# Gated linear attention with a convolved MLP on one core: the scores of all 24 chunks in 64x64 tiles of TensorE

## Chip, cores and metric

One core of a Trainium2 chip runs the whole kernel. The metric is the device time of one execution in microseconds, lower is better.

## What is computed

The reference is a gated linear attention over 4 batches, 8 heads, 768 tokens and 48 channels per head, followed by a three-tap convolution gate in a two-layer network:

```python
f = 1.0 / (1.0 + np.exp(-f_logit))
for t in range(S):
    state = f[:, :, t, :, None] * state + np.einsum('bhd,bhe->bhde', k[:, :, t], v[:, :, t])
    y[:, :, t] = np.einsum('bhd,bhde->bhe', q[:, :, t], state)
# y is laid out as x[b, t, 384], then:
h = np.maximum(x @ w_in, 0.0)                        # 384 -> 1024
conv_out[t] = sum(conv_w[k] * h[t + k - 1] for k in range(3))
out = (h * sigmoid(conv_out)) @ w_out                # 1024 -> 384
```

## The kernel before

The 768 tokens of a batch are cut into 6 chunks of 128, so there are 24 chunks, `n` = 0 to 23. Within a chunk the recurrence becomes matrix products. The running products of the gates scale k and q (`scaled_k`, `scaled_q`); the scores are k times q for every pair of tokens of the chunk; a mask keeps the keys that are not later than the query; the masked scores times v, and the carried state times q, give y. The state is carried on with a product of the turned k (`turned`, a transpose) and v (`state`).

The 8 heads stand in 4 pairs `p` (`NP = 4`); in a pair, head `j = 0` has its 48 channels on partitions 0 to 47 and head `j = 1` on partitions 64 to 111. All of the attention is in plain fp32, and a matmul in fp32 runs as two passes: the trace has two weight loads (LDWEIGHTS) and two MATMUL records for each.

The scores go to the PSUM tile `pa` (128 keys x 2 x 4 x 128 queries) in `scores`. There are two forms, chosen by `NA = 9`:

- For chunks 0 to 8 (line 346) one matmul for each pair and head, with all 128 keys as weights and all 128 queries streamed: 8 matmuls, 16 passes, in two tiles of the array of 64 rows x 128 columns.
- For chunks 9 to 23 (line 353) the 128 keys are cut into four strips of `G = 32`, and each strip is multiplied only with the queries from it on, so that 128, 96, 64 and 32 queries are streamed: 32 matmuls, 64 passes, in eight tiles of 64 rows x 32 columns. In every other pair the keys stand in reversed order (the host lays k and v out so), which puts the strip with 128 queries into the last column tile instead of the first.

VectorE (DVE) then copies the scores under a mask into `am` (`copy_predicated`, lines 357 and 360). For reversed keys the scaling of k must read its factor reversed in every other pair, so `scaled_k` is one DVE operation of 128x512 for chunks 0 to 8 (line 318) and two of 128x256 for the rest (line 321). The parts of `am` of the other pairs that the mask changes over from the one form to the other are cleared on GpSimd (POOL) ahead of chunks 9 and 10 (line 340).

The order of all work is written out by hand in the table `ORDER`: each entry lets one step run on to its next `yield`. The letters that matter here are K (`scaled_k`), a (`scores`: first the matmuls, then the masked copy), y (`values`, line 400: y from the masked scores, then from the state), k (`turned`, line 331), s (`state`, lines 373 and 378), m (`hidden`, line 456: the first layer of the network), r (`result`, lines 495 to 514: the second layer), j (`gated`), and I, J, H, O, P, S, which load and split the weights into two fp32r parts. Each engine works its own list strictly in this order. `pa` has one buffer, and so has the tile `py` that `values` fills.

Of the kernel before, what the change touches and what calls it, by code (L numbers as in the profile page):

```python
# [17 lines left out]
P = 128  # L18
# [1 line left out]

F_MIN = 2.0 ** -64
PN = 6
NA = 9
TS = 24
ON_POOL = ""
ORDER = """
# [10 lines left out]
P1 j0.2 S5 P2 m1.0 m1.0 p8 S0 F12 Q7 j0.0 a7 h1.0 L9 m1.1 s6 K8 S5 L10 s6 m0.7 Q8 m1.0 a7 y6 k8 P1 P1 m1.2 m0.5 m0.7  # L37
m1.3 k8 j0.2 P1 V9 m1.5 m0.6 h1.2 m1.2 m1.2 m0.4 p9 m1.5 m1.3 s7 P2 K9 P4 s7 P1 P4 j0.4 a8 y6 y6 m1.2 P4 P4 S2 m1.3 P1
F13 k9 p9 y7 k9 y7 m1.2 V8 m0.6 m1.4 j0.4 s7 m1.5 a8 m1.7 y7 m1.4 y7 m1.3 m1.4 F14 y8 m1.1 V11 m0.6 m0.7 y8 S1 x12 m1.3
a9 M10 t8 h1.4 L11 m1.5 S2 m1.2 Q9 P4 m1.4 G10 P4 O7 m1.5 P6 P6 a9 s8 j0.6 m1.4 j0.6 y8 S4 y8 h1.6 P6 m1.7 P7 m1.7 m1.2  # L40
s8 P7 m1.6 s8 m1.7 m1.6 M12 m1.6 m1.3 m2.3 p10 m2.3 p10 m2.2 a9 m2.3 m1.6 r0.0 m2.5 m2.2 m1.4 j1.2 L12 K10 r0.1 j1.2
m2.5 m2.2 P6 P6 S1 m2.5 k10 y9 k10 m2.3 m1.5 Q10 S4 a10 s9 m1.7 y9 M13 a10 m2.4 P6 h2.2 P7 P7 S6 m2.2 P7 m2.4 M11 r0.0
t9 r0.0 m1.5 m1.4 S6 j1.4 P7 j1.4 S7 m2.4 S7 m2.5 r0.0 r0.1 m1.1 m1.0 r0.0 y9 r0.0 r0.0 m1.6 r0.1 G11 m1.1 p11 m1.6 r0.1
r0.1 p11 m1.0 m1.0 L13 r0.1 h2.4 t11 m1.6 t10 m1.7 s9 m1.7 m2.4 m2.1 a10 y9 m2.7 r0.1 m2.7 m2.6 r0.2 m2.6 j1.6 j1.0 F15
r0.0 m2.1 r0.2 V10 j1.6 s9 x12 m2.1 Q11 j1.0 K11 G12 m2.7 m2.6 h2.6 m2.4 F17 r0.2 s10 m2.1 r0.5 y10 y10 a11 r0.5 p12 F16
r0.2 m2.6 s10 m2.7 m2.0 h2.0 y10 m2.0 m2.5 m2.0 G14 r0.2 r0.2 x15 m2.4 G13 K12 x15 r0.2 p13 G15 K13 M14 p12 a11 m2.5 p13
s10 r0.5 r0.5 m2.0 r0.1 r0.2 r0.4 m2.2 r0.5 r0.5 V12 m2.1 y10 p14 m2.2 r0.2 r0.4 m2.3 r0.5 m2.2 V13 L14 t12 t13 Q12 Q13
k13 y11 k13 y11 a12 k12 K14 m2.0 m2.6 p15 m2.1 y11 m2.3 r0.2 r0.3 m2.3 m2.1 r0.4 r0.4 y11 m2.5 m2.4 M15 r0.4 r0.4 r0.4
p15 m3.3 r0.4 j2.2 m3.3 m3.2 m3.0 m3.3 k12 a12 V14 a13 y12 m2.0 L15 s12 r0.3 m2.0 j2.4 L16 r0.5 j2.2 m3.0 m3.2 j2.0 m3.0
h3.2 G16 j2.0 a13 y12 m3.2 m2.6 p14 t14 s12 K15 m3.3 m3.1 m3.2 h3.0 m3.1 Q14 j2.4 r0.3 h3.4 r0.3 p16 m2.6 m3.0 m3.1 K16  # L50
F19 m2.7 r0.3 r0.3 m3.1 m2.7 y12 m3.1 L17 m3.4 V16 k14 m2.7 Q15 m3.3 G17 r0.3 r0.3 m3.4 F18 m3.4 m3.7 F20 y13 k14 s13
y13 j2.6 s13 m3.4 y13 y13 a14 k15 p17 j2.6 t15 m3.5 m3.5 r1.0 m3.0 m3.5 K17 m3.5 s13 h3.6 a14 m3.7 m3.7 M18 m3.6 k15
# [30 lines left out]
def gla_moe_kernel(ctx, tc, q_in, k_in, v_in, f_in, w_in, conv_w, w_out, out):  # L83

    nc = tc.nc
# [4 lines left out]
    HP = P // 2  # L90
# [15 lines left out]
    steps = [(b, c) for b in range(B) for c in range(NC)]  # L106
    N = len(steps)
    G = 32
    NB = P // G
    WHOLE = False  # L110
    WHOLE_OUT = 0

# [19 lines left out]
    pa = ps.tile([P, 2, NP, P], F32, name="pa")  # L132
# [183 lines left out]
    def scaled_k(n):  # L316
        if n < NA:
            nc.vector.tensor_tensor(raw["k", n], raw["k", n], fds[n][0], ALU.mult)  # L318
        for i in range(2 if n >= NA else 0):
            k, fi = raw["k", n][:, i::2], fds[n][0][:, i::2]  # L320
            nc.vector.tensor_tensor(k, k, fi[:, :, ::-1] if i else fi, ALU.mult)
        yield
# [13 lines left out]
        yield  # L336

    def scores(n):
        if NA <= n < NA + 2:
            nc.gpsimd.memset(a_b[n % 2][:, :, 1::2], 0.0)  # L340
            yield
        kT, qT = raw["k", n], raw["q", n]
        for p in range(NP if n < NA else 0):
            for j in range(2):
                r = slice(HP * j, HP * j + D)
                nc.tensor.matmul(pa[:, j, p, :], kT[r, p, :], qT[r, p, :], start=True, stop=True)  # L346
        for p in range(NP if n >= NA else 0):
            for i in range(NB):
                t = G * i
                s, o = (P - G - t,) * 2 if p % 2 else (t, t)  # L350
                for j in range(2):
                    r = slice(HP * j, HP * j + D)
                    nc.tensor.matmul(pa[o:o + G, j, p, t:], kT[r, p, s:s + G], qT[r, p, t:],  # L353
                                     start=True, stop=True)
        yield
        if n < NA:
            nc.vector.copy_predicated(a_b[n % 2].rearrange("p j n t -> p (j n) t"), mask0,  # L357
                                      pa.rearrange("p j n t -> p (j n) t"))
        else:
            nc.vector.copy_predicated(a_b[n % 2].rearrange("p j (x y) t -> p (j x) y t", y=2), mask,  # L360
                                      pa.rearrange("p j (x y) t -> p (j x) y t", y=2))
        yield

    def state(n):
        b, c = steps[n]
        kp, vt = kps[n], qkv[n]
        pk = ps.tile([P, NP, HP], F32, tag="s", name=f"pk{n}", bufs=SB)
        for p in range(NP):
            for j in range(2):
                vv = vt[:, p, D * j:D * j + HP].rearrange("p (i e) -> p i e", e=G)  # L370
                vv = vv[:, ::-1] if j else vv
                if n < NA:
                    nc.tensor.matmul(pk[HP * j:HP * j + HP, p, :].rearrange("p (i e) -> p i e", e=G), kp[:, 2 * p + j, :], vv,  # L373
                                     start=True, stop=True)
                    continue
                for x in (0, G):
                    o = HP * j + x
                    nc.tensor.matmul(pk[o:o + G, p, :].rearrange("p (i e) -> p i e", e=G), kp[:, 2 * p + j, x:x + G], vv,  # L378
                                     start=True, stop=True)
        yield  # L380
        old, new = s_b[n % 2], s_b[(n + 1) % 2]
        ft = ft_all[:, b, c, :].rearrange("p (n o) -> p n o", o=1).broadcast_to([P, NP, HP])
        add = pk
        if c > 0:
            add = new
            nc.vector.tensor_tensor(add, pk, old, ALU.add)  # L386
            yield
        (nc.gpsimd if c > 0 else nc.vector).tensor_tensor(new, add, ft, ALU.mult)  # L388
        yield
# [166 lines left out]
    for n, (b, c) in enumerate(steps):  # L556
        todo[f"F{n}"], todo[f"V{n}"] = load_f(n), load_v(n)
        todo[f"L{n}"], todo[f"M{n}"] = load("k", k_in, n), load("q", q_in, n)
        if n < ALONE or n % GC == 0:
            todo[f"x{n}"] = gate(n, 1 if n < ALONE else GC)  # L560
        todo[f"G{n}"], todo[f"p{n}"], todo[f"t{n}"] = summed(n), decays(n), last_decay(n)
        todo[f"K{n}"], todo[f"Q{n}"] = scaled_k(n), scaled_q(n)
        todo[f"a{n}"], todo[f"y{n}"] = scores(n), values(n)
        if c < NC - 1:
            todo[f"k{n}"], todo[f"s{n}"] = turned(n), state(n)
# [15 lines left out]
    with tc.If(known[0] < P * n_ft, label="all_ok"):  # L581
        with ExitStack() as slow:
# [16 lines left out]
            for t0 in range(0, S, TB):  # L599
# [14 lines left out]
                for i in range(B * H):  # L614
                    o = i % 2 * HP
# [27 lines left out]
                for b in range(B):  # L643
                    for h in range(H):
                        src = yb[b * H + h:b * H + h + 1]
                        dst = x_d[b:b + 1, t0:t0 + TB, :].rearrange("o t (k e) -> o t k e", k=KT)
                        o = h // 2 * G
# [82 lines left out]
```

## Time and profile before

| | us |
|---|---|
| median of 3 runs | 305.8 |
| the three runs | 304.39, 305.8, 307.66 |
| the profiled execution | 304.52, of which 302.8 are the span shown in the profile |

| engine | busy us | share of the span |
|---|---|---|
| TensorE, matmuls (PE) | 294.2 | 97% |
| TensorE, weight loads (PEld, beside PE) | 275.6 | 91% |
| VectorE (DVE) | 250.9 | 83% |
| ScalarE (ACT) | 220.4 | 73% |
| GpSimd (POOL) | 82.5 | 27% |

Busy time counts a matmul from the start of its streaming to the modelled end of its results, so records of one engine overlap, and a busy share near one does not say that the array is streaming all the time. A pause of an engine is shown as idle time, with what ended it. The granted clock of TensorE is 1.00 (the 2.4 GHz level) in all slices of the span.

### The profile page before, as it was taken

The page shows a single profiled execution, that of the slowest core. Times are in us where ns is not written, and L with a number is a line of the kernel's source. Part 1 is how long each engine was busy: PE and PEld are TensorE (multiplying, and loading weights), DVE is VectorE, ACT ScalarE, POOL GpSimd, SP SyncE. Part 2 cuts the span into 40 slices and gives each one's busy share as a digit, 9 for nine tenths or more (in the row PEclk, how much of TensorE's full clock was granted, in tenths as well). Part 3 has the DMA queues.
Part 4 walks back from the last instruction along what each step waited for, and adds up shares of the span by engine and source line. Part 5 has one row for each costly group of instructions (what it writes and reads, how often), then busy time and mean ns, then how long its engine had stood idle before and what let it go on. Part 6 is the DMA issues. An engine that isn't in the chain of part 4 may idle for free.

```text
span 302.8 us, 9854 instructions
## 1 busy us (share of the span) xinstructions
PE 294.2 (97%) x4227; PEld 275.6 (91%) x4227; DVE 250.9 (83%) x380; ACT 220.4 (73%) x422; POOL 82.5 (27%) x107
## 2 busy tenths in 40 slices
PE   7799999999999999999999999999999999999994
PEld 5678888889999899999999999999999999999994
DVE  4999999999999999877999999946893976479520
ACT  4999999889968986767976995664756544676521
POOL 4466874454403140400232410230305010000000
PEclk9999999999999999999999999999999999999999
DMA  7999961283026502736315230602012000000211
GB/s 225 395 397 394 403 219 35 84 305 110 0 73 163 142 20 68 187 119 205 102 32 171 64 124 4 195 2 81 6 36 83 2 28 28 28 1 0 81 54 55
DMA packets 19378, 35.73 MB, mean 118 GB/s; under 512 B 2156, under 2 KB 9092, under 8 KB 19332
## 3 DMA queue, kind: packets, MB, share of 16 engines
q1 hardware_dynamic: 19044, 34.69, 34.1%
q8 instruction: 34, 0.56, 0.7%
q10 hardware_dynamic: 288, 0.39, 0.3%
q14 instruction: 12, 0.10, 0.1%
HBM read 30.35 MB, written 4.72 MB: 116 GB/s over the span
## 4 chain that ended last, share of the span: by engine, by line
PE 79%; DVE 6%; issue 1%; ACT 0%; DVEq 0%
PE po L509 33%; PE ph L456 28%; PE py L400 8%; PE pa L353 4%; PE ptk L331 2%; PE pk L378 2%; DVE am L357 1%; DVE g L466 1%; DVE g L468 1%; DVE fb L298 0%; DVE wol L196 0%; DVE k L318 0%; DVE wil L196 0%; PE pk L373 0%; PE pa L346 0%
## 5 line engine op out<-in xcount | busy, mean ns | idle before, releaser
L456 PE MATMUL ph<-xT,wih 128*128 128x384 f32 x384 | 99.8, 340 | 0.0
L456 PEld LDWEIGHTS ph<-xT,wih 128*128 128x128 f32 x384 | 68.3, 188 | 1.3 <-ACT hb L459 0.4
L509 PE MATMUL po<-woh,gh 128*128 128x384 f32 x192 | 64.7, 337 | 0.0
L456 PE MATMUL ph<-xT,wil 128*128 128x384 f32 x192 | 64.3, 335 | 0.0
L509 PE MATMUL po<-woh,gl 128*128 128x384 f32 x192 | 64.2, 334 | 0.0
L509 PE MATMUL po<-wol,gh 128*128 128x384 f32 x192 | 64.2, 334 | 0.0
L466 DVE SCALAR_TENSOR_TENSOR g<-hb,cw,g 128x384 f32<-128x384 f32 (+1 forms) x64 | 41.3, 653 | 13.1 <-ACT g L464 12.8
L468 DVE SCALAR_TENSOR_TENSOR g<-hb,cw,g 128x384 f32<-128x384 f32 (+1 forms) x64 | 41.7, 668 | 0.7
L459 ACT ACTIVATE hb<-ph 128x384 f32<-128x384 f32 x64 | 30.7, 487 | 11.5 <-PE ph L456 10.9
L464 ACT ACTIVATE g<-hb,cw 128x384 f32<-128x384 f32 (+1 forms) x64 | 38.0, 615 | 0.3
L497 DVE TENSOR_TENSOR gl<-g,gh 128x1024 fp32r<-128x1024 f32 (+4 forms) x34 | 30.3, 906 | 9.4 <-ACT gh L495 9.4
L325 POOL TENSOR_TENSOR q<-q,fd 128x512 f32<-128x512 f32 x19 | 28.4, 1497 | 34.0 <-ACT fd L308 29.2
L509 PEld LDWEIGHTS po<-woh,gh 128*128 128x128 f32 x192 | 36.0, 188 | 0.4 <-issue 0.2
L509 PEld LDWEIGHTS po<-wol,gh 128*128 128x128 f32 x192 | 36.0, 188 | 0.0
L509 PEld LDWEIGHTS po<-woh,gl 128*128 128x128 f32 x192 | 36.0, 188 | 0.0
L456 PEld LDWEIGHTS ph<-xT,wil 128*128 128x128 f32 x192 | 36.0, 188 | 0.0
L495 ACT CAST gh<-g 128x1024 fp32r<-128x1024 f32 (+4 forms) x34 | 26.5, 801 | 13.0 <-PE po L509 9.2
L477 DVE SCALAR_TENSOR_TENSOR g<-g,hb 128x768 f32<-128x768 f32 (+1 forms) x32 | 30.1, 951 | 3.9 <-ACT g L475 3.9
L514 ACT COPY ob<-po 128x384 f32<-128x384 f32 x24 | 11.3, 475 | 29.9 <-PE po L509 27.8
L388 POOL TENSOR_TENSOR st<-st,ft_all 128x256 f32<-128x256 f32 x16 | 17.3, 1080 | 50.3 <-DVE st L386 50.2
L475 ACT ACTIVATE g<-g 128x768 f32<-128x768 f32 (+1 forms) x32 | 26.7, 847 | 4.0 <-DVE g L468 4.0
L313 POOL COPY ft_all<-fd 128x4 f32<-128x4 f32 x24 | 11.0, 465 | 56.1 <-ACT fd L308 56.1
(92 smaller groups left out, 459.5 us busy)
## 6 DMA issues: line engine op xcount, KB each, us to landing
k<-in_k_dram SPq DMA_DIRECT2D x24, 256.0 KB, 4.2
q<-in_q_dram SPq DMA_DIRECT2D x24, 256.0 KB, 4.6
v<-in_v_dram SPq DMA_DIRECT2D x24, 224.0 KB, 4.6
fb<-in_f_logit_dram SPq DMA_DIRECT2D x18, 256.0 KB, 4.3
out_dram<-ob SPq DMA_DIRECT2D x22, 192.0 KB, 2.3
wis<-in_moe_w_in_dram SPq DMA_DIRECT2D x6, 512.0 KB, 6.2
wos<-in_moe_w_out_dram SPq DMA_DIRECT2D x8, 384.0 KB, 5.9
fb<-in_f_logit_dram SPq DMA_DIRECT2D x6, 200.0 KB, 5.1
```

Source lines behind the costliest of these rows:

```text
L325: (nc.vector if n < QV else nc.gpsimd).tensor_tensor(raw["q", n], raw["q", n], fds[n][1], ALU.mult)
L400: nc.tensor.matmul(py[G * p:G * p + G, t, :], lhs, rhs, start=start, stop=stop)
L456: nc.tensor.matmul(ph, w, xts[b, hf][:, t, xl, :], start=(k == 0), stop=(k == 3 * KT - 1))
L459: nc.scalar.activation(hb[:, 2:HS + 2], ph, AF.Relu, scale=0.5)
L464: nc.scalar.activation(cv, hb[:, 1:n + 1], AF.Copy, scale=cw[:, 1, f:f + 1])
L466: nc.vector.scalar_tensor_tensor(cv, hb[:, 2:n + 2], cw[:, 2, f:f + 1], cv, ALU.mult, ALU.add)
L468: nc.vector.scalar_tensor_tensor(cv, hb[:, 0:n], cw[:, 0, f:f + 1], cv, ALU.mult, ALU.add)
L475: nc.scalar.activation(cv, cv, AF.Tanh)
L477: nc.vector.scalar_tensor_tensor(cv, cv, 1.0, h_b[:, fp:fp + 2, 1:n + 1], ALU.add, ALU.mult)
L495: nc.scalar.copy(hi, g[:, f:f + k])
L497: nc.vector.tensor_tensor(lo, g[:, f:f + k], hi.bitcast(F32), ALU.subtract)
L509: nc.tensor.matmul(po, g[:, f, :], w, start=(i == 0), stop=(i == 3 * NF - 1))
```

## The change

`NA` becomes 0, so that all 24 chunks take the second form, and that form is cut differently: two strips of 64 keys instead of four of 32. A strip is multiplied with the queries from it on (128 or 64), and stands in the upper or the lower 64 columns of the array, in the other half for every other pair. A chunk has 16 matmuls (32 passes) in four tiles of 64 rows x 64 columns.

With it, k and v are laid out reversed in every other pair for chunks 0 to 8 too (on the host), `scaled_k` has two operations for all chunks, the masked copy of all chunks goes by line 360's form, and the two clearings on POOL go, with one `a9` and one `a10` in `ORDER` (all lines of the table behind them are only filled anew). The state's products keep their two forms, with the border at chunk 9 (`n < 9` for `n < NA`). The branch that computes everything again, which was not taken in the trace, reads k and v by `NA` too.

```diff
-NA = 9
+NA = 0
@@ ORDER @@
-a9 M10 t8 h1.4 L11 m1.5 ...
+M10 t8 h1.4 L11 m1.5 ...
-... K10 r0.1 j1.2
-m2.5 m2.2 P6 P6 S1 m2.5 k10 y9 k10 m2.3 m1.5 Q10 S4 a10 s9 m1.7 ...
+... K10 r0.1 j1.2 m2.5
+m2.2 P6 P6 S1 m2.5 k10 y9 k10 m2.3 m1.5 Q10 S4 s9 m1.7 ...
@@ gla_moe_kernel @@
-    NB = P // G
@@ scores @@
-        if NA <= n < NA + 2:
+        if 0 < NA <= n < NA + 2:
             nc.gpsimd.memset(a_b[n % 2][:, :, 1::2], 0.0)
             yield
@@
         for p in range(NP if n >= NA else 0):
-            for i in range(NB):
-                t = G * i
-                s, o = (P - G - t,) * 2 if p % 2 else (t, t)
+            for t in (0, HP):
+                o = HP - t if p % 2 else t
                 for j in range(2):
                     r = slice(HP * j, HP * j + D)
-                    nc.tensor.matmul(pa[o:o + G, j, p, t:], kT[r, p, s:s + G], qT[r, p, t:],
+                    nc.tensor.matmul(pa[o:o + HP, j, p, t:], kT[r, p, o:o + HP], qT[r, p, t:],
                                      start=True, stop=True)
@@ state @@
-                if n < NA:
+                if n < 9:
```

On TensorE, the place of the scores of chunk 9, behind `values` of chunk 7 (before):

```order
L400 MATMUL py_1144<-am_75,v_1117 32x128 x16
L400 MATMUL py_1144<-q_782,st_77 32x128 x12
L353 MATMUL pa<-q_914,k_960 32x128 x2
L353 MATMUL pa<-q_914,k_960 32x96 x2
L353 MATMUL pa<-q_914,k_960 32x64 x2
L353 MATMUL pa<-q_914,k_960 32x32 x2
```

The same place with the change (buffers have other numbers, lines stand one or two higher up):

```order
L454 MATMUL ph_4_1201<-xT_1_675,wih 128x384 x2
L454 MATMUL ph_4_1201<-xT_1_675,wil_1_752 128x384
L398 MATMUL py_1225<-am_75,v_1198 32x128 x16
L398 MATMUL py_1225<-q_836,st_77 32x128 x12
L351 MATMUL pa<-q_978,k_1032 64x128 x2
L351 MATMUL pa<-q_978,k_1032 64x64 x2
```

The four rows of line 353 (one pair) come four times in a chunk, those of line 351 too: 32 matmuls have become 16, at the same place.

On TensorE, the scores of chunk 8 between `state` of chunk 7 and `turned` of chunk 9, before:

```order
L373 MATMUL pk_1042<-v_832,kp_80 64x64 x8
L346 MATMUL pa<-q_782,k_773 128x128 x8
L331 MATMUL ptk_1079<-ident,k_960 128x128 x4
L400 MATMUL py_1085<-am_76,v_832 32x128 x16
L400 MATMUL py_1085<-q_911,st_78 32x128 x12
```

The end of the same scores and what follows, with the change:

```order
L351 MATMUL pa<-q_836,k_827 64x128 x2
L351 MATMUL pa<-q_836,k_827 64x64 x2
L330 MATMUL ptk_1160<-ident,k_1032 128x128 x4
L398 MATMUL py_1166<-am_76,v_887 32x128 x16
L398 MATMUL py_1166<-q_975,st_78 32x128 x12
```

Eight matmuls of 128 queries have become sixteen, half of them of 64 queries; the neighbours are the same.

On DVE, the scaling of k of chunk 6 (`k_487`, and `k_515` with the change), before and after:

```order
L468 SCALAR_TENSOR_TENSOR g_674<-hb,cw,g_674 128x384
L318 TENSOR_TENSOR k_487<-k_487,fi_692 128x512
L430 TENSOR_TENSOR xT_1_630<-py_729,xT_1_630 128x3x128
L466 SCALAR_TENSOR_TENSOR g_674<-hb,cw,g_674 128x384
L188 SCALAR_TENSOR_TENSOR mswo_670<-mswo_670 128x384
```

```order
L466 SCALAR_TENSOR_TENSOR g_720<-hb,cw,g_720 128x384
L320 TENSOR_TENSOR k_515<-k_515,fi_738 128x2x128 x2
L428 TENSOR_TENSOR xT_1_675<-py_783,xT_1_675 128x3x128
L464 SCALAR_TENSOR_TENSOR g_720<-hb,cw,g_720 128x384
L187 SCALAR_TENSOR_TENSOR mswo_716<-mswo_716 128x384
```

One row has become two; nothing on DVE has changed its place. This holds at all nine chunks 0 to 8.

## Rows read from the trace of the kernel before

**Rows 1.** Two stretches: length, busy PE, PEld, DVE, ACT, POOL, granted clock, DMA share, GB/s

```profile
8.50:58.40 49.90, 48.42 (x790) 41.87 (x786) 49.62 (x78) 48.25 (x100) 29.02 (x35) 1.00 0.73 274
...
65.40:100.00 34.60, 34.60 (x562) 32.62 (x561) 34.56 (x54) 29.69 (x57) 11.46 (x16) 1.00 0.32 101
```

**Rows 2.** Timeline, all engines: start us, length us, engine, line, records, [idle before <-releaser]

```profile
58.85 0.33 PE L331 MATMUL ptk<-ident,k 128*128 128x128 f32 x1 [0.32 <-DVE st L388]
...
65.38 0.70 PEld L400 LDWEIGHTS py<-am,v 128*32 128x32 f32 x28 [0.17 <-DVE xT L430]
```

**Rows 3.** Waits from 65.6 us on: what waited, for whom, us in total, times, longest

```profile
PE pa L353 <- issue: 0.5, 2, 0.3
...
PEld pk L378 <- DVE am L360: 0.2, 1, 0.2
```

**Rows 4.** Timeline of PE: scores of a chunk and the group behind them, three places

```profile
63.70 1.16 PE L346 MATMUL pa<-q,k 48*128 48x128 f32 x16
64.80 0.66 PE L331 MATMUL ptk<-ident,k 128*128 128x128 f32 x4
...
71.27 0.99 PE L353 MATMUL pa<-q,k 48*32 48x128 f32 x64
72.19 0.28 PE L373 MATMUL pk<-v,kp 128*64 128x64 f32 x2
...
122.02 1.00 PE L353 MATMUL pa<-q,k 48*32 48x128 f32 x64
122.95 0.52 PE L400 MATMUL py<-am,v 128*32 128x128 f32 x9
```

**Rows 5.** Timeline of PE in short stretches: records of single passes, lines 346 and 373

```profile
63.25 0.40 PE L373 MATMUL pk<-v,kp 128*64 128x64 f32 x8
...
63.54 0.23 PE L373 MATMUL pk<-v,kp 128*64 128x64 f32 x2
...
63.92 0.50 PE L346 MATMUL pa<-q,k 48*128 48x128 f32 x5
...
64.59 0.27 PE L346 MATMUL pa<-q,k 48*128 48x128 f32 x1
```

**Rows 6.** Instructions of lines 346 and 373: duration in ns, min/median/max

```profile
L346 PE MATMUL pa<-q,k x144: 272/272/373, 9.3 to 64.6; 48*128 48x128 f32 x144
...
L373 PE MATMUL pk<-v,kp x128: 219/222/270, 16.9 to 72.7; 128*64 128x64 f32 x128
```

**Rows 7.** Timeline of PE: the products of line 400 ahead of the scores

```profile
49.53 0.78 PE L400 MATMUL py<-q,st 128*32 128x128 f32 x24
50.24 0.38 PE L346 MATMUL pa<-q,k 48*128 48x128 f32 x2
...
70.69 0.78 PE L400 MATMUL py<-q,st 128*32 128x128 f32 x24
```

**Rows 8.** Timeline of DVE: the scaling of k in one operation and in two

```profile
45.67 0.67 DVE L318 TENSOR_TENSOR k<-k,fi 128x512 f32<-128x512 f32 x1
46.27 0.54 DVE L430 TENSOR_TENSOR xT<-py,xT 128x384 fp32r<-128x384 f32 x1
...
106.30 0.73 DVE L321 TENSOR_TENSOR k<-k,fi 128x256 f32<-128x256 f32 x2
106.95 1.21 DVE L298 TENSOR_TENSOR_SCAN fb<-going,fb 128x512 f32<-128x512 f32 x1
```

**Rows 9.** Timeline of PE: scores of two chunks, and the group behind them

```profile
100.37 0.60 PE L353 MATMUL pa<-q,k 48*32 48x128 f32 x29
...
101.70 0.45 PE L456 MATMUL ph<-xT,wih 128*128 128x384 f32 x1
...
143.97 0.96 PE L353 MATMUL pa<-q,k 48*32 48x128 f32 x50
...
145.47 0.44 PE L331 MATMUL ptk<-ident,k 128*128 128x128 f32 x2
```

**Rows 10.** The page's DMA queues: packets, MB, share of 16 engines

```profile
q8 instruction: 34, 0.56, 0.7%
```

More of the change, by code (lines that the diff above doesn't have):

```diff
@@ L39 @@
 F13 k9 p9 y7 k9 y7 m1.2 V8 m0.6 m1.4 j0.4 s7 m1.5 a8 m1.7 y7 m1.4 y7 m1.3 m1.4 F14 y8 m1.1 V11 m0.6 m0.7 y8 S1 x12 m1.3
[L40 to L48, printed above, removed]
@@ L49 @@
-p15 m3.3 r0.4 j2.2 m3.3 m3.2 m3.0 m3.3 k12 a12 V14 a13 y12 m2.0 L15 s12 r0.3 m2.0 j2.4 L16 r0.5 j2.2 m3.0 m3.2 j2.0 m3.0
+M10 t8 h1.4 L11 m1.5 S2 m1.2 Q9 P4 m1.4 G10 P4 O7 m1.5 P6 P6 a9 s8 j0.6 m1.4 j0.6 y8 S4 y8 h1.6 P6 m1.7 P7 m1.7 m1.2 s8
+P7 m1.6 s8 m1.7 m1.6 M12 m1.6 m1.3 m2.3 p10 m2.3 p10 m2.2 a9 m2.3 m1.6 r0.0 m2.5 m2.2 m1.4 j1.2 L12 K10 r0.1 j1.2 m2.5
+m2.2 P6 P6 S1 m2.5 k10 y9 k10 m2.3 m1.5 Q10 S4 s9 m1.7 y9 M13 a10 m2.4 P6 h2.2 P7 P7 S6 m2.2 P7 m2.4 M11 r0.0 t9 r0.0
+m1.5 m1.4 S6 j1.4 P7 j1.4 S7 m2.4 S7 m2.5 r0.0 r0.1 m1.1 m1.0 r0.0 y9 r0.0 r0.0 m1.6 r0.1 G11 m1.1 p11 m1.6 r0.1 r0.1
@@ new lines @@
+p11 m1.0 m1.0 L13 r0.1 h2.4 t11 m1.6 t10 m1.7 s9 m1.7 m2.4 m2.1 a10 y9 m2.7 r0.1 m2.7 m2.6 r0.2 m2.6 j1.6 j1.0 F15 r0.0
+m2.1 r0.2 V10 j1.6 s9 x12 m2.1 Q11 j1.0 K11 G12 m2.7 m2.6 h2.6 m2.4 F17 r0.2 s10 m2.1 r0.5 y10 y10 a11 r0.5 p12 F16 r0.2
+m2.6 s10 m2.7 m2.0 h2.0 y10 m2.0 m2.5 m2.0 G14 r0.2 r0.2 x15 m2.4 G13 K12 x15 r0.2 p13 G15 K13 M14 p12 a11 m2.5 p13 s10
+r0.5 r0.5 m2.0 r0.1 r0.2 r0.4 m2.2 r0.5 r0.5 V12 m2.1 y10 p14 m2.2 r0.2 r0.4 m2.3 r0.5 m2.2 V13 L14 t12 t13 Q12 Q13 k13
+y11 k13 y11 a12 k12 K14 m2.0 m2.6 p15 m2.1 y11 m2.3 r0.2 r0.3 m2.3 m2.1 r0.4 r0.4 y11 m2.5 m2.4 M15 r0.4 r0.4 r0.4 p15
@@ L50 @@
+m3.3 r0.4 j2.2 m3.3 m3.2 m3.0 m3.3 k12 a12 V14 a13 y12 m2.0 L15 s12 r0.3 m2.0 j2.4 L16 r0.5 j2.2 m3.0 m3.2 j2.0 m3.0
 h3.2 G16 j2.0 a13 y12 m3.2 m2.6 p14 t14 s12 K15 m3.3 m3.1 m3.2 h3.0 m3.1 Q14 j2.4 r0.3 h3.4 r0.3 p16 m2.6 m3.0 m3.1 K16
```

## Prediction

> **What bounds the kernel now.** I read first the busy time by stage, then the waits, then the timeline at the scores themselves. From 8.5 to 58.4 us VectorE works 49.62 of 49.90 us while TensorE's records cover 48.42 [rows 1]: both are full, but VectorE does not pause, and TensorE is the one that waits. The end of that stage shows it: at 58.85 us the transposes of line 331 have waited for VectorE's line 388, and at 65.38 us the products of line 400 for VectorE's line 430 [rows 2]. So up to about 65 us the list of VectorE sets the time. This stretch holds all nine chunks of the first form (the last of them starts at 63.70, [rows 4]). From there on it is TensorE: in 65.4 to 100 us its records cover all 34.60 us [rows 1], and in all the time after 65.6 us the waits for another engine are single ones, 0.2 us for the masked copy, say. What else stands there against `pa` is 0.5 us in two pauses that no engine ended [rows 3]. A microsecond of TensorE saved before 65 us should therefore be worth nothing, a microsecond added to VectorE there its full length, and after 65 us TensorE's work counts in full.
>
> **What a chunk's scores cost now.** The clock of TensorE is granted in full in all of this (the 1.00 in [rows 1]), so durations can be carried from one place to another. A chunk of the first form lasts 1.10 us from its start to that of the group behind it (63.70 to 64.80), one of the second form 0.92 (71.27 to 72.19), or 0.93 (122.02 to 122.95) [rows 4]. The 1.10 come apart like this. A short stretch of the timeline shows the passes alive in it, and its row starts with the oldest. Line 346 has 16 passes in two tiles, eight steps; the second step starts at 63.92 and the eighth at 64.59, so a pass of 128 queries takes 0.67/6 = 0.112 us, and the two tiles run side by side. Line 373 streams 64 columns in two tiles: third step 63.25, eighth 63.54, so 0.29/5 = 0.058 us a pass [rows 5]. The first pass of a group also waits for its weights: 373 ns against 272 for 128 columns of weights, 270 against 222 for 64, so 0.10 and 0.05 us [rows 6]. From the last step (64.59) to the next group (64.80) are 0.21 us: one pass and 0.10 us of emptying the array. Together 0.10 + 8 x 0.112 + 0.10 = 1.10, which is what the rows show.
>
> **What it costs with the change.** In the 64x64 form each of the four tiles gets, over four pairs, four passes of 128 queries and four of 64, since the order turns round from pair to pair: 4 x 0.112 + 4 x 0.058 = 0.68 us, if a tile that has finished early goes on with the next pair. With 0.05 for the weights and 0.10 for emptying that is 0.83 us.
>
> Chunks 0 to 8: 1.10 - 0.83 = 0.27 us less on TensorE each, 2.4 us in all, and at nothing, because VectorE's list covers it. What would be gained if the cover were gone is a rival below.
>
> Chunks 9 to 23: 0.09 us less each (0.10 by the 0.93), but the way in changes. Thirteen of these fifteen follow `values`, whose last products are in tiles of 64 rows x 32 columns, as the scores now are. There the scores start at 71.27, 0.20 us before the modelled end of those products (70.69 + 0.78 = 71.47). Where another shape of tiles follows them, it starts at 50.24, 0.07 before that end (49.53 + 0.78 = 50.31) [rows 4, 7]. So a change of shape costs 0.13 us, and the new form pays it: 0.13 - 0.09 = +0.04 us for each of thirteen, +0.5 us. The other two follow the big matmuls of the network (one is the 122.02), have paid that already, and win 0.10 us each, -0.2. Together +0.3 us, all in the stretch where TensorE counts in full. The Trainium skill has this as a rule that speaks against the change ("TensorEngine Tiling (Array Packing)", Key Properties: a change of the tiling mode, not merely of the tile, drains TensorE). It gives no price; the trace agrees, with 0.13 us.
>
> VectorE: in nine chunks one operation becomes two. The one takes 0.60 us until the next starts (45.67 to 46.27), the two 0.65 (106.30 to 106.95) [rows 8]: +0.05, nine times, +0.4 us, at the engine that sets the pace there. By their own durations without overlap the two would be 0.73 against 0.67, which is much the same; the reversed reading is already in the rows of the two. The masked copies keep shape and time, and the two clearings on POOL go from an engine that the waits after 65.6 us do not name, so 0 for both. No transfer changes its size or place.
>
> The two pauses: the scores of the chunk at 100.37 last 1.33 us until the next group (101.70) and those at 143.97 last 1.50 (145.47), against 0.92 elsewhere [rows 4, 9]: 0.41 + 0.58 = 1.0 us, put down to "issue", that is, to nothing the trace shows. One queue of 34 packets and 0.56 MB brings instructions, 16 KB at a time [rows 10]. A chunk's scores of line 353 use up 128 instructions (64 loads, 64 matmuls) in 0.92 us, the densest piece of the program, and both pauses lie inside such a piece. I take them for TensorE running out of instructions. With 64 instead of 128 in the same time both should go: -1.0 us; the bounds are 0 (they stay, or come at other places) and -1.0.
>
> Sum: +0.3 + 0.4 - 1.0 = -0.3 us against the profiled execution (304.52). That one and the three runs (304.39, 305.8, 307.66) have their middle at 305.2, 0.6 below the median of the three; from this level the change gives **304.9 us**. With the single values between 304.39 and 307.66, about 1% is what a measurement of this kernel can tell from no change.
>
> **The rivals.**
> (B) The tiles don't run ahead into the next pair. The form of 32 columns speaks for it: per tile it streams, over four pairs, only two times 128 + 32 and two times 96 + 64, so by the rate of 0.112 us for 128 columns about 4 x (0.112 + 0.028) = 0.56 us, yet its 0.92 us are nearly those of 8 passes of 128 [rows 4]. It seems that the reversal does not pay there and each pair lasts as long as its longest tile. If the new form is like that, its middle is 8 x 0.112 = 0.90 instead of 0.68, a chunk 1.05 us, and thirteen chunks cost 0.13 + 0.13 = +0.26 each, two +0.12: +3.6; with +0.4 and -1.0 the sum is +3.0, 308.2 us, slower than before. Against it: with four tiles there are 32 passes to keep track of and not 64, and a tile needs only one matmul of lead. It decides from a middle of 0.70 us on: 13 x (0.13 + 0.70 + 0.15 - 0.92) + 2 x (0.70 + 0.15 - 0.93) + 0.4 - 1.0 is zero.
> (C) TensorE sets the pace before 65 us as well, and VectorE is only just kept busy. For it: TensorE is covered to 97% there. Against it: it is TensorE that waits. Then 9 x 0.27 = 2.4 us come in full and VectorE's 0.4 are hidden: -2.4 + 0.3 - 1.0 = -3.1, 302.1 us.
> (D) The change from 32 to 64 columns with the same rows does not empty the array. Then the thirteen lose nothing on the way in and hide the 0.05 of the weights: -0.14 each, -1.8; with -0.2 + 0.4 - 1.0 the sum is -2.6, 302.6 us. The rows of 50.24 change the rows too, so they do not exclude it.
> (E) The pauses have another cause, or the blocks of instructions now end at other dense places: +0.3 + 0.4 = +0.7, 305.9 us. The Trainium skill ("Runtime: NRT & Kernel Launch", Instruction fetch mechanics) says that instructions come in blocks of 16 KiB ahead of use, and that crossing a block is mostly hidden. By that rule this case follows; the trace agrees on the size of the blocks, and its two pauses speak against "hidden".
>
> **How the numbers follow.** Forecast 0.53, B 0.16, C 0.10, D 0.06, E 0.13, 0.02 for the rest. The forecast's own terms (0 to -1.0 for the pauses, 0.05 to 0.2 us per scaling, which is the difference of two full durations at their slowest) and the scatter of the runs give it 303.9 to 306.2. To leave out no more than 2 in 10 the range goes from 302.4 (D and the upper part of C) to 308.0 (the lower half of B). Faster by over 1% is under 302.7: C, half of D and a little of the forecast, 0.12. Slower by over 1% is over 308.9: the upper part of B, 0.08. The rest, 0.80, lies within 1%.
>
> **What would show it.** In the profile after: the scores of a chunk at 0.83 us from start to next group; 0.13 us between `values` and the scores that was not there; in 8.5 to 58.4 us VectorE still without a pause, TensorE with about 2 us more of waiting, above all at the transposes and at line 400; the transposes that stood at 58.85 now at about 59.2; no pause "issue" inside the scores. Scores of 1.05 us would show B; the transposes of that place before 58 us, C; a start of the scores 0.20 us before the end of the products, D; a pause within the scores or within line 400, E. The forecast is wrong if the transposes at 58.85 move earlier, or if the stretch from there to the end changes by more than 1.5 us.

## The result, and the profile after

The changed kernel takes 307.94 us (median of 20 runs, 306.82 to 311.03), the kernel before 305.27 us in the same session (20 runs, 304.36 to 308.56). The ratio is 1.0072 with a 95% interval of 1.0049 to 1.0095: slower, where 304.9 us, a little faster, was forecast.

| | before | after |
|---|---|---|
| profiled execution | 304.52 us | 307.90 us |
| its span | 302.8 us | 306.2 us |
| start of the transposes that wait for VectorE's `st` near 59 us | 58.85 us | 62.78 us |
| from there to the end | 243.95 us | 243.42 us |
| busy PE | 294.2 us | 295.0 us |
| busy DVE | 250.9 us | 254.5 us |
| busy POOL | 82.5 us | 78.9 us |

The table already says where to look. The stretch in which TensorE sets the time became 0.53 us shorter; the stretch before it became 3.93 us longer. VectorE is busy 3.6 us more, and GpSimd 3.6 us less. The next rows are of the changed kernel: the stage table for the stretch of [rows 1] (length, busy PE, PEld, DVE, ACT, POOL, granted clock, DMA share, GB/s), and TensorE's timeline at the transposes of [rows 2].

```profile
8.50:58.40 49.90, 45.63 (x832) 38.02 (x829) 49.45 (x78) 45.39 (x93) 24.43 (x34) 0.97 0.75 273
```

```profile
62.78 0.33 PE L330 MATMUL ptk<-ident,k 128*128 128x128 f32 x1 [0.65 <-DVE st L386]
```

VectorE is still without a pause (49.45 of 49.90 us) and the transposes still wait for it, but VectorE reaches them 3.9 us later. Its list has only one kind of new operation, so the scaling of k comes first. This is the scaling of chunk 1 in the kernel before, with what stands beside it on GpSimd: the timeline of DVE, and below the dots that of POOL.

```profile
10.58 0.69 DVE L318 TENSOR_TENSOR k<-k,fi 128x512 f32<-128x512 f32 x1
11.19 1.33 DVE L357 COPY_PREDICATED am<-mask,pa 128x1024 f32<-128x1024 uint8 x1
...
10.73 1.05 POOL L180 TENSOR_SCALAR mswi<-wis 128x512 f32<-128x512 f32 x1 [2.26 <-DVE wi L190]
```

And the same place after the change: the second half of the scaling, the masked copy, and GpSimd.

```profile
10.88 0.87 DVE L320 TENSOR_TENSOR k<-k,fi 128x256 f32<-128x256 f32 x1
...
11.68 1.31 DVE L358 COPY_PREDICATED am<-mask,pa 128x1024 f32<-128x1024 uint8 x1
...
10.71 0.76 POOL L179 TENSOR_SCALAR mswi<-wis 128x512 f32<-128x512 f32 x1 [3.02 <-DVE wi L189]
```

Read the two durations of GpSimd's clamp against each other. Before, it is recorded from 10.73, while the scaling runs until 11.27, and lasts 1.05 us. After, it lasts 0.76 us, and the second half of the scaling, 0.41 us elsewhere, lasts 0.87 us. It looks as if one of the two engines waits for the other inside its own operation: before it was GpSimd that waited, and nobody waited for GpSimd; now it is VectorE. The waiting shows as a longer duration, not as idle time, so no view of waits names it.

The other long operations of VectorE after the change, each with the GpSimd operation that was running:

```profile
17.24 0.88 DVE L320 TENSOR_TENSOR k<-k,fi 128x256 f32<-128x256 f32 x1
...
17.08 0.75 POOL L179 TENSOR_SCALAR mswi<-wis 128x512 f32<-128x512 f32 x1
...
38.68 1.80 DVE L195 TENSOR_TENSOR wil<-wi,wih 128x512 fp32r<-128x512 f32 x1
...
38.44 1.49 POOL L324 TENSOR_TENSOR q<-q,fd 128x512 f32<-128x512 f32 x1
...
49.33 0.83 DVE L320 TENSOR_TENSOR k<-k,fi 128x256 f32<-128x256 f32 x1
...
49.09 0.79 POOL L386 TENSOR_TENSOR st<-st,ft_all 128x256 f32<-128x256 f32 x1
```

Take off VectorE's undisturbed duration from its end (0.41 us for a half, 0.67 for line 195): it would have begun at 11.34, 17.71, 39.81 and 49.75. The GpSimd operations are recorded as ending at 11.47, 17.83, 39.93 and 49.88. In all four VectorE begins when GpSimd is done (0.12 to 0.13 us ahead of the recorded end).

From the start of the scaling to the next operation on VectorE, chunk by chunk:

| chunk | 0 | 1 | 2 | 3 | 4 | 5 | 6 | 7 | 8 |
|---|---|---|---|---|---|---|---|---|---|
| before, us | 0.91 | 0.61 | 0.60 | 0.58 | 0.61 | 0.60 | 0.60 | 0.60 | 0.60 |
| after, us | 0.91 | 1.13 | 1.39 | 1.51 | 1.01 | 1.03 | 1.09 | 0.67 | 0.67 |

The sum is 3.70 us more (0.19 of it, in chunk 2, is a wait for ScalarE). That leaves 0.2 of the 3.93: line 195 at 38.68 and another operation at 47.89 lost 0.75 and 0.58 us more than before, and three that GpSimd had held up before ran freely now and won 0.30 to 0.45 us each.

TensorE did what the forecast said. These rows answer [rows 4, 7, 9]: the products ahead of the scores, the scores, the group behind them, of a chunk with the way in from 32 columns, one behind the big matmuls, and the one that had held the longer pause.

```profile
74.48 0.78 PE L398 MATMUL py<-q,st 128*32 128x128 f32 x24
75.19 0.90 PE L351 MATMUL pa<-q,k 48*64 48x128 f32 x32
76.02 0.69 PE L371 MATMUL pk<-v,kp 128*64 128x64 f32 x16
...
125.69 0.90 PE L351 MATMUL pa<-q,k 48*64 48x128 f32 x32
126.52 0.64 PE L398 MATMUL py<-am,v 128*32 128x128 f32 x16
...
147.75 0.90 PE L351 MATMUL pa<-q,k 48*64 48x128 f32 x32
148.58 0.66 PE L330 MATMUL ptk<-ident,k 128*128 128x128 f32 x4
```

The scores of each of the chunks 9 to 23 last 0.83 us from start to the next group. Behind `values` they begin 0.07 us before the modelled end of the products (74.48 + 0.78 = 75.26), where the old form began 0.20 before it: the 0.13 us of the forecast. Neither pause is there.

### The profile page after: what moved, and what is told of

It reads as the page before. It is cut to its first block, busy times and chain, and to the rows that moved or that the text cites. A ratio compares the mean times of both kernels' runs of the same rounds, so it can differ in the third digit from the quotient of the medians.

```text
span 306.2 us, 9189 instructions
## 1 busy us (share of the span) xinstructions
PE 295.0 (96%) x3891; PEld 272.5 (89%) x3891; DVE 254.5 (83%) x389; ACT 220.8 (72%) x422; POOL 78.9 (26%) x105
## 4 chain that ended last, share of the span: by engine, by line
PE 78%; DVE 6%; issue 1%; ACT 0%
PE po L507 33%; PE ph L454 28%; PE py L398 8%; PE pa L351 4%; PE ptk L330 2%; PE pk L376 2%; DVE g L466 1%; DVE fb L297 1%; DVE k L320 1%; DVE g L464 1%; DVE am L358 1%; DVE mswo L187 0%; DVE xT L428 0%; DVE wol L195 0%; PE pk L371 0%
## 5 line engine op out<-in xcount | busy, mean ns | idle before, releaser
L358 DVE COPY_PREDICATED am<-mask,pa 128x1024 f32<-128x1024 uint8 x24 | 31.9, 1328 | 2.0 <-PE pa L351 1.8
```

## The experiments

Three theories stood for the 3.7 us. **Split**: the scaling, cut in two, lets GpSimd in between the halves, and the second half waits. **Reversal**: reading the factors backwards is slow. **Form**: the 64x64 scores shift the engines against each other, and the long operations are a consequence.

**Only the split, in the kernel before.** Two halves in chunks 0 to 8, not reversed, all else as before:

```diff
-        if n < NA:
-            nc.vector.tensor_tensor(raw["k", n], raw["k", n], fds[n][0], ALU.mult)
-        for i in range(2 if n >= NA else 0):
+        for i in range(2):
             k, fi = raw["k", n][:, i::2], fds[n][0][:, i::2]
-            nc.vector.tensor_tensor(k, k, fi[:, :, ::-1] if i else fi, ALU.mult)
+            nc.vector.tensor_tensor(k, k, fi[:, :, ::-1] if i and n >= NA else fi, ALU.mult)
```

> The kernel before with one edit: in chunks 0 to 8 the scaling of k is two operations of two pairs each, neither of them reversed; scores, order and layout of the data are those of before. (Split) If cutting the operation in two is what costs, because GpSimd gets in between the halves: the second half takes 0.75 to 0.88 us instead of 0.42 in five or six of the nine chunks, VectorE loses about 3 us before 65 us, and the time is 308.2 us (1.008 to 1.012 of before). (Reversal) If reading backwards is what costs: all halves at 0.39 to 0.43 us, 305.7 us. (Form) If the 64x64 scores themselves move the work against each other: 305.7 us too.

308.36 us against 305.47, ratio 1.0100 (1.0063 to 1.0136). Timelines of DVE, POOL and PE:

```profile
10.77 0.88 DVE L319 TENSOR_TENSOR k<-k,fi 128x256 f32<-128x256 f32 x1
...
10.60 0.76 POOL L180 TENSOR_SCALAR mswi<-wis 128x512 f32<-128x512 f32 x1 [2.48 <-DVE wi L190]
...
61.96 0.33 PE L329 MATMUL ptk<-ident,k 128*128 128x128 f32 x1 [0.36 <-DVE st L386]
```

The second half is as long as with the reversal, and in five chunks (1, 2, 4, 5, 6): 0.88, 0.95, 0.76, 0.75, 0.83 us. Chunk 3 escapes here, as GpSimd starts later there; line 196, directly behind it, pays instead: 1.15 us in place of 0.67. The transposes come 3.1 us late. The 0.8 us to the 3.9 of the changed kernel lie in single places: the wait for ScalarE in chunk 2 and what follows from it (0.3), chunk 3, which is hit there in both halves (0.4), and the start of the list (0.1). So the split alone makes the loss, without reversal and without the new scores. Reversal and Form fall.

**The change without the split.** ScalarE writes the factors of every other pair reversed, so that VectorE needs one operation:

```diff
-        nc.scalar.activation(fi, fv, AF.Exp)
+        if n < 9:
+            nc.scalar.activation(fi[:, 0::2], fv[:, 0::2], AF.Exp)
+            nc.scalar.activation(fi[:, 1::2, ::-1], fv[:, 1::2], AF.Exp)
+        else:
+            nc.scalar.activation(fi, fv, AF.Exp)
 ...
-        if n < NA:
+        if n < 9:
             nc.vector.tensor_tensor(raw["k", n], raw["k", n], fds[n][0], ALU.mult)
```

> The changed kernel with one edit: in chunks 0 to 8 ScalarE writes the factors of every other pair already reversed (two operations instead of one), so that VectorE scales k in one operation again; scores in 64x64 tiles in all chunks. (Split) and (Reversal): the 3.5 us before the transposes of 59 us are gone, those stand at 58.6 to 59.4 again, the later stretch keeps its gain of 0.5, and the time is 304.8 us (0.996 to 1.000 of before). (Form) The time stays at 307.5 to 308 us, with single VectorE operations still 0.4 us too long.

304.65 us, ratio 0.9969 (0.9948 to 0.9990). The timelines of DVE and PE, and the stage table for the stretch of [rows 1]:

```profile
10.44 0.69 DVE L321 TENSOR_TENSOR k<-k,fi 128x512 f32<-128x512 f32 x1
...
58.74 0.33 PE L334 MATMUL ptk<-ident,k 128*128 128x128 f32 x1 [0.56 <-DVE st L390]
```

```profile
8.50:58.40 49.90, 46.61 (x914) 39.91 (x910) 49.59 (x78) 48.51 (x108) 29.59 (x35) 1.00 0.73 274
```

All nine scalings are back at 0.66 to 0.69 us, the transposes at 58.74, and the 3.9 us are gone. The rows also show what TensorE's saving is worth before 65 us: it is busy 1.8 us less there than in [rows 1], and the transposes move by 0.1, no more than this profile's first scaling starts earlier (7.35 for 7.61).

**The new scores in chunks 9 to 23 only**, the rest as before:

```diff
-            for i in range(NB):
-                t = G * i
-                s, o = (P - G - t,) * 2 if p % 2 else (t, t)
+            for t in (0, HP):
+                o = HP - t if p % 2 else t
 ...
-                    nc.tensor.matmul(pa[o:o + G, j, p, t:], kT[r, p, s:s + G], qT[r, p, t:],
+                    nc.tensor.matmul(pa[o:o + HP, j, p, t:], kT[r, p, o:o + HP], qT[r, p, t:],
```

> The kernel before with one edit: only chunks 9 to 23 have their scores in 64x64 tiles, chunks 0 to 8 stay as they were. (Split), (Reversal) and (Form) all give the stretch before 58.85 us unchanged; if the later stretch was read rightly (0.04 us more per chunk with a way in from 32 columns, 0.10 less for two, no pause inside the scores) it is 0.5 to 0.7 us shorter, 304.7 us (0.996 to 1.000 of before). Rival: the gain of the later stretch in the changed kernel came from its shifted start and not from the scores; then 305.3 us or more.

304.26 us, ratio 0.9965 (0.9937 to 0.9992): a third of a per cent faster, like the kernel just before. The profiled execution (305.92 us) lies above that. Its early stretch is 1.5 us longer than before, and TensorE ran at half clock in 8 to 12 us (below); from its transposes to the end it takes 304.1 - 60.39 = 243.7 us:

```profile
60.39 0.33 PE L330 MATMUL ptk<-ident,k 128*128 128x128 f32 x1 [0.28 <-DVE st L386]
```

That stretch is 243.7 us in the kernel without the split as well (302.4 - 58.74). But it is 243.6 with the old scores too, in the kernel with only the split (305.6 - 61.96), and 243.95 before. So the gain after 59 us rests on the medians of the two kernels, and on them only in its direction; in single profiles it lies within what one differs from the next.

**The disputed cost by itself.** A list of VectorE operations and one clamp on GpSimd, each clamp released by the VectorE operation of line 86 ahead of the scaling. Per round, in short form:

```python
nc.vector.tensor_tensor(w, w, m, ALU.mult)              # line 86, releases the clamp
nc.gpsimd.tensor_scalar(m, hw, 4.0, -4.0, ALU.min, ALU.max)   # line 51, with or without
half(0); half(1, reversed or not)                       # line 42; line 38 whole; line 45 one input
other(); other(); other()                               # line 48, an input in PSUM
```

> Not the kernel, but the disputed cost alone (the output is filled with a constant): VectorE's list of a two-input operation that releases a GpSimd clamp of 128x512, then k times factors in six ways (whole; two halves; two halves, the second reversed; two halves with another operation that has an input in PSUM between them; factors in PSUM; halves with one input), four times with the clamp and four times without. (Split) With the clamp the second half takes 0.75 to 0.9 us, reversed or not, and the whole operation 0.6 to 0.7; with an input in PSUM, and without the clamp, nothing is lengthened. (Reversal) Only the reversed half is long, and without the clamp as well. The two remaining ways (another operation between the halves, halves with one input) are open: if a half with a single input waits too, the cost does not hang on the second operand.

Rows of DVE and POOL: the whole operation with the clamp, two halves with it (the second one alone), the reversed half, two halves without the clamp, and a half with one input.

```profile
8.43 0.68 DVE L38 TENSOR_TENSOR k<-k,fi 128x512 f32<-128x512 f32 x1
...
8.60 1.02 POOL L51 TENSOR_SCALAR m<-raw 128x512 f32<-128x512 f32 x1 [2.23 <-DVE w L86]
...
35.31 0.86 DVE L42 TENSOR_TENSOR k<-k,fi 128x256 f32<-128x256 f32 x1
...
35.14 0.75 POOL L51 TENSOR_SCALAR m<-raw 128x512 f32<-128x512 f32 x1 [3.02 <-DVE w L86]
...
49.60 0.75 DVE L42 TENSOR_TENSOR k<-k,fi 128x256 f32<-128x256 f32 x2
...
63.66 0.86 DVE L42 TENSOR_TENSOR k<-k,fi 128x256 f32<-128x256 f32 x1
...
143.20 0.75 DVE L45 TENSOR_SCALAR k<-k 128x256 f32<-128x256 f32 x1
...
143.17 0.64 POOL L51 TENSOR_SCALAR m<-raw 128x512 f32<-128x512 f32 x1 [2.23 <-DVE w L86]
```

Instructions of the two ways of halving (duration in ns, min/median/max; `pf` is the copy of the factors in PSUM):

```profile
L42 DVE TENSOR_TENSOR k<-k,fi x48: 415/418/861, 31.2 to 111.2; 128x256 f32<-128x256 f32 x48
L42 DVE TENSOR_TENSOR k<-k,pf x16: 412/414/416, 113.4 to 137.0; 128x256 f32<-128x256 f32 x16
```

This is one execution, with four rounds of each kind. The whole operation keeps its 0.68 us, and the clamp takes 1.02. With halves the clamp takes 0.75, and the second half 0.86 instead of 0.42, whether it is read backwards (63.66) or not (35.31), in all eight rounds, and only with the clamp. That repeats the two pictures of chunk 1 to within 0.03 us. With the factors in PSUM no half is lengthened in 16, and the clamp takes 0.64 us. With another operation that has an input in PSUM between the halves both take 0.42 us. A half with a single input, 0.29 us otherwise, waits as well (0.75), in three rounds of four; in the first the clamp waited. So a second operand is not needed for a collision. This is Split, with a cause: these operations of VectorE and one of GpSimd that reads SBUF don't run side by side, one waits for the whole of the other. The Trainium skill says the same ("SBUF — State Buffer", Who interferes with whom): a port pair shared by the two engines is locked for a whole instruction, and a VectorE instruction with two inputs in SBUF contends for it with a GpSimd instruction that reads SBUF. These runs agree, at 0.44 us a collision.

**The split kept, the halves taken apart.** If GpSimd's turn comes at the end of the first half, an operation that doesn't contend, put there, should run in the meantime. In chunks 1, 2, 4 and 6 the second half moves behind the next operation in VectorE's list, of chunk 1 for example:

```diff
-I2.0 c p1 x2 G2 H0.0 K1 c a0 x3 J1.0
+I2.0 c p1 x2 G2 H0.0 K1 c a0 K1 x3 J1.0
 ...
             nc.vector.tensor_tensor(k, k, fi[:, :, ::-1] if i else fi, ALU.mult)
+            if i == 0 and n in (1, 2, 4, 6):
+                yield
```

> The changed kernel with one edit in VectorE's list: in chunks 1, 2, 4 and 6 the second half of the scaling of k stands one operation later, behind the masked copy or the xT subtraction that followed it, which have an input in PSUM; all work stays, GpSimd's too. (Split, GpSimd gets in between the halves) GpSimd's operation runs beside the one with the input in PSUM; these four second halves fall from 871, 880, 751 and 831 ns to 0.55 us or less, 1.3 to 1.8 us in all; the transposes at 62.78 us come at 61.0 to 61.5, the time is 306.0 to 306.6 us (307.9 for the changed kernel), as far as no other operation of VectorE with two inputs in SBUF is hit instead. (Half) If a second half is slow in itself, they stay at 0.75 to 0.88 us and the time at 307.9 us. (TensorE) If the scores, now released up to 1.3 us later, set the time, it is over 308 us.

306.32 us, ratio 1.0035 (1.0008 to 1.0063), in the range that Split gave. Timelines of DVE, POOL and PE:

```profile
10.76 0.42 DVE L320 TENSOR_TENSOR k<-k,fi 128x256 f32<-128x256 f32 x1
11.09 1.32 DVE L360 COPY_PREDICATED am<-mask,pa 128x1024 f32<-128x1024 uint8 x1
12.30 0.41 DVE L320 TENSOR_TENSOR k<-k,fi 128x256 f32<-128x256 f32 x1
...
10.92 0.76 POOL L179 TENSOR_SCALAR mswi<-wis 128x512 f32<-128x512 f32 x1 [2.88 <-DVE wi L189]
...
21.61 0.73 DVE L320 TENSOR_TENSOR k<-k,fi 128x256 f32<-128x256 f32 x2
...
60.83 0.44 PE L332 MATMUL ptk<-ident,k 128*128 128x128 f32 x2 [0.63 <-DVE st L388]
```

The clamp runs beside the masked copy, which keeps its 1.32 us, and the second half takes 0.41. In chunks 2 and 6 it takes 0.46 and 0.41 us; in chunk 4 still 0.69, more than the 0.55 expected, because GpSimd's next operation, line 181 (31.50 to 32.01), stands just ahead of it. Together the four save 1.36 us; the transposes come at 60.83 instead of 62.78, somewhat before the 61.0 that was the lower end. The scores, which get their k up to 1.2 us later, do not set the time. One operation was hit in their place, line 187 at 17.83 (1.10 us instead of 0.67). Chunk 3, which the edit does not touch, escapes in this profile too (21.61: both halves together 0.73 us, 1.58 in the changed kernel); that makes up most of the rest of the 1.95 us, so the edit itself accounts for the 1.36 less the 0.4 of line 187.

**One operation in all 24 chunks**: the kernel without the split, with the reversed writing by ScalarE and the single scaling in chunks 9 to 23 too (`if True:` in place of `if n < 9:`).

> The changed kernel with the scaling of k in one operation in all 24 chunks (ScalarE writes the factors of every other pair reversed everywhere, not in chunks 0 to 8 alone). VectorE saves 15 times up to 0.05 us, and once 0.8 us where a half now waits for GpSimd, all after 65 us. If TensorE alone sets the time there: 304.6 us, within 0.3 of the kernel with this edit in chunks 0 to 8. If VectorE's list counts there as well: 303.5 to 304.0 us. If the second operation on ScalarE counts: 305.0 us or more.

304.83 us, ratio 1.0001 (0.9974 to 1.0028), within 0.2 us of the kernel with that edit in chunks 0 to 8 only. The halves cost about 0.07 us in each of chunks 9 to 23, so some 1 us of VectorE's work after 65 us shows no effect on the time, as it must be where TensorE sets it. The one collision there, in chunk 14, did not go, against the expectation: the whole operation waits at the same place (timeline of DVE). What a collision costs after 65 us was therefore not tested.

```profile
128.09 1.45 DVE L320 TENSOR_TENSOR k<-k,fi 128x512 f32<-128x512 f32 x1
```

## Why the prediction was wrong

- **The step that failed** is the price of the split on VectorE: "+0.05, nine times, +0.4 us", taken from the pair at 106.30 [rows 8]. In 104.9 to 108 us of that trace GpSimd has no operation at all, so that row is a price without a neighbour. The eight scalings of chunks 1 to 8 cost 3.70 us more, not 0.4: two at 0.07, near the forecast, and six at 0.40 to 0.93. The upper bound (0.2 us each, "the difference of two full durations at their slowest") rested on the same row. The trace of before showed what a collision costs, at a single half of a later chunk beside GpSimd's scaling of q, and also halves that meet GpSimd's clamp and lose nothing, in chunk 9 (timelines of DVE and POOL):

```profile
127.77 1.18 DVE L321 TENSOR_TENSOR k<-k,fi 128x256 f32<-128x256 f32 x1
...
127.06 1.61 POOL L325 TENSOR_TENSOR q<-q,fd 128x512 f32<-128x512 f32 x1
...
62.93 0.75 DVE L321 TENSOR_TENSOR k<-k,fi 128x256 f32<-128x256 f32 x2
...
63.09 0.98 POOL L180 TENSOR_SCALAR mswo<-wos 128x384 f32<-128x384 f32 x1 [2.88 <-DVE wo L190]
```

  The first row is a first half, and a whole scaling waits at that place too (128.09 above), so it prices a collision and not the cut. Still, with an upper bound of 0.8 us (1.18 - 0.41) for a half that meets GpSimd, the range would have reached some 7 us higher by this estimate, and the case would have been a rival of its own.
- **What would have pointed to the chunks at risk** are GpSimd's rows in the trace of before. In chunks 1, 2, 4, 5 and 6 an operation of GpSimd starts during the scaling of k and takes 1.05, 1.05, 0.92, 0.90 and 1.06 us, where the same kinds take 0.64, 0.54 and 0.61 us undisturbed: it waits for the scaling already. With the change it starts during the first half and goes first at the cut. It is no sure sign: chunk 3 has no such row and was hit, and chunks 8 and 9, where GpSimd's operation is longer as well (2.12 us for the scaling of q, 0.98 for the clamp), lose nothing to it. The forecast asked what the two operations last, not what stands beside them in the 8.5 to 58.4 us where GpSimd works 29.02 us [rows 1].
- **That VectorE sets the time up to about 65 us** was right: its 3.70 us came through, as 3.93; and TensorE's saving there was worth 0.1 us when it stood alone. Rival C falls.
- **The scores** were right: 0.83 us a chunk, 0.13 us on the way in. Rival B (1.05 us a chunk) and rival D (no emptying) fall. This forecast's slower rival, B, gave about the time that was measured by a mechanism that isn't there.
- **The pauses** left the scores, as forecast, and in none of the kernels with 64x64 scores in these chunks does one lie inside them. That they belong to fixed places is not so: with the same instructions of TensorE as before, the kernel with only the split has a pause in the chunk at 146.62 (the old 143.97) and one at 167.61, where there was none, and none in the chunk of the old 100.37; its two chunks are 0.42 and 0.32 us over the 0.92 elsewhere, of which up to 0.1 at the second is a wait of the transposes for VectorE (the starts of the scores and of the group behind them in TensorE's timeline):

```profile
146.62 1.40 PE L351 MATMUL pa<-q,k 48*32 48x128 f32 x64
147.96 0.44 PE L329 MATMUL ptk<-ident,k 128*128 128x128 f32 x2
...
167.61 1.31 PE L351 MATMUL pa<-q,k 48*32 48x128 f32 x64
168.85 0.55 PE L329 MATMUL ptk<-ident,k 128*128 128x128 f32 x3
```

  What causes the pauses was not tested; that TensorE runs out of instructions there stays a guess. The instruction packets fell from 34 to 31 [rows 10].
- **The stretch from the transposes to the end** was to change by +0.3 - 1.0 = -0.7 us and changed by -0.53; against the other profiles it is between 0 and -0.5, as told above.

The sum with the measured terms is +3.93 - 0.53 = +3.40, the difference of the two spans; the medians of the runs differ by 2.7.

## What to carry to other kernels

Before one operation of VectorE is cut in two at an engine that sets the pace, look at GpSimd beside it: the cut is a place where a waiting GpSimd operation can go first, and then the second half waits for all of it. That cost 0.4 to 0.9 us a chunk here, in six of the eight chunks 1 to 8. If it must be cut, put an operation with an input in PSUM between the pieces, keep one input of the pieces in PSUM, or let another engine prepare the data so that no cut is needed; the last gave 304.65 us here. Take a duration only from a row that has the same neighbours as the place to which it is carried.

## What the hardware showed that was not expected

- Waiting for the other engine stands inside the recorded duration, on both sides. The clamp of 128x512 takes 0.64 us when free, 0.75 behind a half, 1.02 behind a whole scaling; the half takes 0.42 or 0.86. The busy time of an engine then counts its waiting: VectorE's 3.6 us more are mostly waiting. That GpSimd's busy time fell by the same 3.6 us is chance in part: 1.06 us of it are the two clearings, and in the kernel with only the split, where VectorE is busy 3.3 us more, GpSimd's 82.4 us are those of before.
- A run of operations on VectorE does not always keep GpSimd out, and not always lets it in. In chunks 1, 2, 4 and 5 and in the list made for it the waiting clamp went first at the cut. In chunk 9 the clamp's 0.98 us (63.09 above) reach past both halves, which keep their 0.75 together; and in the changed kernel GpSimd's scaling of q waits through the halves of chunk 8 (timelines of POOL and DVE; it takes 1.31 us elsewhere). What decides who goes first is not shown by these runs.

```profile
60.68 2.85 POOL L324 TENSOR_TENSOR q<-q,fd 128x512 f32<-128x512 f32 x1 [3.36 <-ACT fd L307]
...
61.17 0.76 DVE L320 TENSOR_TENSOR k<-k,fi 128x256 f32<-128x256 f32 x2
```

- TensorE's clock fell early in some profiles. In the changed kernel its granted clock was 0.57 in 14 to 18 us, in the kernel with the late scores only it was 0.57 in 8 to 12 us; the stage tables of the two:

```profile
14.00:18.00 4.00, 4.00 (x87) 2.99 (x81) 4.00 (x7) 2.39 (x6) 2.50 (x4) 0.57 1.02 389
```

```profile
6.00:8.00 2.00, 0.00 (x0) 0.00 (x0) 0.43 (x1) 1.48 (x4) 1.71 (x4) 1.00 1.04 395
8.00:12.00 4.00, 3.98 (x34) 3.54 (x35) 3.12 (x6) 3.55 (x8) 1.69 (x3) 0.57 1.04 380
```

  For the most part of these stretches that is the lower level of 1.2 GHz. In the second kernel TensorE had stood still for 2 us just before; in the first it had waited 0.86 and 0.92 us shortly before, at 11.60 and 13.62. In the profile of the kernel with only the split the clock is 1.00 throughout and the transposes still come 3.1 us late, and six of the 20 runs of the changed kernel have a clock of 1.00 and take 306.87 to 307.94 us. So the clock is not what made the change slower.
